# Block attention and feed-forward: another order of scores, attn*v and transposes in the pairs of batches 2 to 7

## The chip, the cores and the metric

The kernel runs on one core of one Trainium2 chip. The time is that of one execution on the device in microseconds (us); lower is better.

## The reference

Attention over q, k, v of 8 batches, 8 heads, 576 positions and 64 columns with a block mask (blocks of 64; a block sees itself and those before it), then a feed-forward part on all 4608 rows with 512 and 2048 columns. All is float32.

```python
scores = scale * np.matmul(q, k.transpose(0, 1, 3, 2))
mask = block_i >= block_j                     # block = position // 64
scores = np.where(mask, scores, -1000000000.0)
scores = scores - np.max(scores, axis=-1, keepdims=True)
attn = np.exp(scores)
attn = attn / (np.sum(attn, axis=-1, keepdims=True) + 1e-09)
x = np.matmul(attn, v)                        # then (B*S, H*D)
h = x @ w_in
g = np.where(h >= 1, h, np.where(h <= -1, 0.0, (h + 1) ** 2 / 4))
out = g @ w_out
```

## The kernel before

**Tiling.** Two heads make a pair, so there are 32 pairs, four to a batch. Each value is held as two float32r parts (high and low), and products are made of several matmuls of such parts. `q` and `k` of a pair are transposed on TensorE into `qa`, `qb`, `ka`, `kb` (`turned_raw`, L401, for the 512 main positions of one head; `turned_last`, L442, for the last 64 of both heads). `parted` takes four reads to split a bank of them (L388 ScalarE, L389 VectorE, L394 ScalarE, L395 VectorE); `turned_last` has two more on VectorE (L446).

**One pair.** `scores(j, g)` makes softmax rows of head j, group g (query tiles 0 and 1; 2; 3): matmuls L482 and L485 into a bank, the maximum L505 (VectorE), the exponential L509 (ScalarE), sum and reciprocal L491 and L492, and the scaling L515 into `pr`. `scores_last` does the last 64 rows of both heads. `as_float32r` then copies `pr` by DMA to `prr` in the float32r type (L250, queue SP). `turn(j, g)` transposes `prr` (L552), and `split` reads the bank twice (L545 ScalarE, L547 VectorE) into `pa` (group 0) or `pb`. `turn_last` does so for the last rows; their last 64 columns, the corner of P, have a transpose, a bank and two reads of their own, into `pcs`. attn*v are the matmuls L591: `attn_v_first` for the first 256 rows of both heads, `attn_v(0)` and `attn_v(1)` for the other 320 rows of one head. `add_halves` copies half of the bank to `xtmp` (L613 ScalarE) and adds the other (L614 VectorE) into `x32`, which `store_x` splits into `xh` and `xl` for the feed-forward part.

**Order.** `attention_steps` gives eight steps per pair, with `old`, `cur` and `nxt` the pair before, this one and the one behind. The pairs of batches 2 to 7 are `far`, `raw` and `hop`; those before are laid out otherwise. From step 36 on each attention step is followed by one step of `feed_forward`: `ffn_in` (twelve matmuls L770 of 512 columns into `ph`; then L779 ScalarE, L780 and L783 VectorE, L784 ScalarE, L785 GpSimd) in the odd steps 1, 3, 5, 7, and `ffn_out` (twelve matmuls L794 and L799) in the even ones. So the far pairs run, with what follows in each step:

| step | before, in the source's order | feed-forward |
|---|---|---|
| 0 | old.turn(1, 1), scores(0, 0), load v, old.attn_v_first | ffn_out |
| 1 | old.turn(1, 2), scores(0, 1), turned_last, fetch | ffn_in |
| 2 | old.attn_v(1), old.store_x, scores(0, 2) | ffn_out |
| 3 | begin, turn(0, 0), scores_last, nxt.load_qk | ffn_in |
| 4 | turn(0, 1), scores(1, 0), nxt QK of half 0 | ffn_out |
| 5 | turn(0, 2), scores(1, 1) | ffn_in |
| 6 | turn_last with the corner, scores(1, 2) | ffn_out |
| 7 | turn(1, 0), attn_v(0), nxt QK of half 1 | ffn_in |

**Banks.** PSUM has eight banks: four for `po`, one for `ph`, and in this stretch three for all the rest (`work_bank`, L85, `bufs=3`). Waits between engines are put in by the framework. It also lays out each engine's queue when the program is built, with the source's order as its guide; the trace shows where the two differ.

## Time and profile before

| | before |
|---|---|
| median of 3 runs | 1267.56 us (1264.57 to 1269.79) |
| the profiled execution | 1269.69 us, span 1267.9 us |
| mean granted TensorE clock | 0.981 of 2.4 GHz |
| busy: TensorE / VectorE / ScalarE / GpSimd | 95% / 70% / 55% / 31% |
| weight loads of TensorE | 79% |
| the 16 DMA engines | 54.9% for the data queue |

The far pairs take from about 262 to about 1075 us. From 1086 us on the feed-forward part runs alone. In the rows, PE is TensorE, DVE VectorE, ACT ScalarE, POOL GpSimd, SPq the SP queue that issues DMAs; L numbers are lines of the kernel. A matmul's row ends later than the next one's starts, since matmuls are pipelined; what a matmul costs the queue is the time from its start to the next start.

### The profile page before, as it was taken

The numbers are of one execution on the slowest core, as the hardware profiler recorded it, in microseconds if no ns is written. First come the engines' busy times: TensorE is split into PE (matmuls) and PEld (weight loads), VectorE is DVE, ScalarE is ACT, GpSimd is POOL, SyncE is SP. The second block draws the span as 40 slices with busy tenths as digits, with TensorE's granted clock in tenths as the row PEclk, the third lists the DMA queues.
The fourth block names the chain that finished last, engine by engine and source line by source line (L and its number), as shares of the span: only waits on it lengthen the run. The fifth ranks groups of instructions, "written<-read, shape, count | busy, mean of one in ns | idle before, by whom it ended". The sixth has DMA issues, their size and how long they took to land.

```text
span 1267.9 us, 20253 instructions
## 1 busy us (share of the span) xinstructions
PE 1200.1 (95%) x6280; PEld 998.8 (79%) x6280; DVE 887.0 (70%) x2188; ACT 703.2 (55%) x1827; POOL 394.6 (31%) x430
## 2 busy tenths in 40 slices
PE   5888889899999999999999999999999999999998
PEld 4666667678888888888888888888888888888886
DVE  8898877758777777777777777787777777322222
ACT  5787656646566655665656655566556555222222
POOL 3555655522222222222222222222222222222222
PEclk9888988999999999999999999999999999999999
DMA  5566666667888655555554655465556433422432
GB/s 158 167 176 215 203 228 197 217 198 237 260 273 266 215 162 158 154 175 163 156 162 145 187 157 152 138 189 153 160 154 190 137 128 118 132 87 98 133 100 100
DMA packets 185259, 215.43 MB, mean 170 GB/s; under 512 B 113840, under 2 KB 132272, under 8 KB 184384
## 3 DMA queue, kind: packets, MB, share of 16 engines
q1 hardware_dynamic: 185152, 214.14, 54.9%
q8 instruction: 50, 0.82, 0.3%
q14 instruction: 57, 0.47, 0.1%
HBM read 134.74 MB, written 31.98 MB: 131 GB/s over the span
## 4 chain that ended last, share of the span: by engine, by line
PE 69%; DVE 16%; ACT 6%; issue 5%; DMA 1%; POOL 1%; SPq 1%; ACTq 0%; POOLq 0%; DVEq 0%
PE ph L770 29%; PE po L794 15%; PE po L799 7%; PE ps_av L591 7%; PE ps_s L482 4%; ACT pr L509 3%; PE ps_s L485 3%; DVE t L780 2%; PE ps_t L552 2%; DVE t L783 2%; ACT t L779 2%; DVE pb L547 2%; DVE nm L505 2%; DVE sm L491 1%; DVE pr L515 1%
## 5 line engine op out<-in xcount | busy, mean ns | idle before, releaser
L785 POOL TENSOR_TENSOR gl<-t,gh 128x512 fp32r<-128x512 f32 x144 | 187.5, 1302 | 510.2 <-ACT gh L784 333.2
L794 PE MATMUL po<-wo,gh 128*128 128x512 f32 x1152 | 296.1, 397 | 0.5 <-DMA wo<-wo_split 0.3
L794 PEld LDWEIGHTS po<-wo,gh 128*128 128x128 f32 x1152 | 212.5, 189 | 44.5 <-DMA wo<-wo_split 0.7
L770 PE MATMUL ph<-xh,wih 128*128 128x512 f32 x576 | 232.9, 404 | 1.6 <-DVE t L783 1.6
L770 PE MATMUL ph<-xh,wil 128*128 128x512 f32 x576 | 228.8, 397 | 0.0
L770 PE MATMUL ph<-xl,wih 128*128 128x512 f32 x576 | 227.8, 396 | 0.5 <-DVE xl L627 0.5
L780 DVE SCALAR_TENSOR_TENSOR t<-t 128x512 f32<-128x512 f32 x144 | 101.5, 705 | 168.0 <-ACT t L779 165.2
L779 ACT ACTIVATE t<-ph 128x512 f32<-128x512 f32 x144 | 85.9, 597 | 173.8 <-PE ph L770 173.8
L509 ACT ACTIVATE pr<-ps_s,nm 128x128 f32<-128x128 f32 (+3 forms) x256 | 134.1, 527 | 60.5 <-DVE nm L505 58.4
L784 ACT CAST gh<-t 128x512 fp32r<-128x512 f32 x144 | 89.5, 621 | 120.3 <-DVE t L783 120.0
L799 PE MATMUL po<-wo,gl 128*128 128x512 f32 x576 | 155.6, 392 | 0.0
L482 PE MATMUL ps_s<-ka,qa 68*128 68x288 f32 (+4 forms) x384 | 135.3, 367 | 15.0 <-ACT pr L509 5.4
L379 POOL TENSOR_TENSOR vsr<-vn,vsr 128x256 fp32r<-128x256 f32 (+1 forms) x96 | 55.2, 576 | 246.2 <-ACT vsr L378 244.6
L770 PEld LDWEIGHTS ph<-xh,wil 128*128 128x128 f32 x576 | 109.5, 190 | 23.8
L770 PEld LDWEIGHTS ph<-xh,wih 128*128 128x128 f32 x576 | 109.8, 191 | 21.7 <-DVE t L783 2.3
L799 PEld LDWEIGHTS po<-wo,gl 128*128 128x128 f32 x576 | 108.7, 189 | 23.1
L505 DVE TENSOR_REDUCE nm<-ps_s 128x1 f32<-128x128 f32 (+3 forms) x256 | 118.8, 482 | 10.4 <-PE ps_s L485 9.4
L770 PEld LDWEIGHTS ph<-xl,wih 128*128 128x128 f32 x576 | 109.7, 190 | 20.5 <-DVE xl L627 0.9
L485 PE MATMUL ps_s<-kb,qb 128*128 128x288 f32 (+4 forms) x384 | 121.1, 322 | 0.0
L515 DVE TENSOR_SCALAR pr<-pr,sm 128x128 f32<-128x128 f32 (+3 forms) x256 | 107.3, 440 | 5.4
L783 DVE TENSOR_TENSOR t<-ph,t 128x512 f32<-128x512 f32 x144 | 98.7, 686 | 2.2
L491 DVE TENSOR_SCALAR sm<-sm 128x1 f32<-128x1 f32 (+1 forms) x224 | 52.0, 232 | 68.3 <-ACT pr L509 65.7
(111 smaller groups left out, 1871.4 us busy)
## 6 DMA issues: line engine op xcount, KB each, us to landing
wo<-wo_split SPq DMA_DIRECT2D x144, 512.0 KB, 3.5
prr<-pr SPq DMA_DIRECT2D x96, 192.0 KB, 2.5
prr<-pr SPq DMA_DIRECT2D x72, 256.0 KB, 2.8
out_dram<-ob SPq DMA_DIRECT2D x36, 256.0 KB, 2.9
bits<-in_moe_w_in_dram SPq DMA_DIRECT2D x32, 256.0 KB, 3.5
bits<-in_moe_w_out_dram SPq DMA_DIRECT2D x32, 256.0 KB, 3.0
wo_split<-ws SPq DMA_DIRECT2D x16, 512.0 KB, 2.9
qa<-qb SPq DMA_DIRECT2D x63, 128.0 KB, 2.4
```

The lines of the kernel that those rows point to most:

```text
L482: nc.tensor.matmul(ps, qa[:KA, j, c0 : c0 + P], ka[:KA, j, k0 : k0 + n], start=first, stop=False)
L485: nc.tensor.matmul(ps, qb[:, j, c0 : c0 + P], kb[:, j, k0 : k0 + n], start=False, stop=last)
L505: nc.vector.tensor_reduce(out=nm[:, i : i + 1], in_=ps[:, cs], axis=AX.X, op=ALU.max, negate=True)
L509: nc.scalar.activation(pr[:, cs], ps[:, cs], AF.Exp, bias=nm[:, i : i + 1], scale=1.0, accum_out=sm[:, i : i + 1],)
L515: nc.vector.tensor_scalar_mul(pr[:, cs], pr[:, cs], sm[:, i : i + 1])
L770: nc.tensor.matmul(ph, w[:, cc, fs], x[:, cc, xs], start=(cc == 0 and i == 0), stop=(cc == NCC - 1 and i == 2),)
L779: nc.scalar.activation(t_, ph, AF.Relu, bias=0.5, scale=0.5)
L780: nc.vector.scalar_tensor_tensor(out=t_, in0=t_, scalar=1.0, in1=t_, op0=ALU.min, op1=ALU.mult)
L783: nc.vector.tensor_tensor(out=t_, in0=ph, in1=t_, op=ALU.max)
L785: nc.gpsimd.tensor_tensor(out=gl, in0=t_, in1=gh.bitcast(F32), op=ALU.subtract)
L794: nc.tensor.matmul(po[tt], gh[:, ts_], wo[:, w, :], start=(fc == 0 and w == 0), stop=False)
L799: nc.tensor.matmul(po[tt], gl[:, ts_], wo[:, 0, :], start=False, stop=fc == NFC - 1)
```

## The change

For the pairs of batches 2 to 7 alone: in each step the scores come first, then the transposes or attn*v. `attn_v(0)` moves from step 7 to step 0 of the next pair, and `attn_v_first` from step 0 to step 1, with one `xtmp` for its two halves; `attn_v(1)` stays in step 2. `turned_last` of the next pair runs in step 5 and no more in the pair's own step 1. The corner of P is transposed in step 7 into the free columns of the bank of `turn(1, 0)`, and no more in step 6 into a bank of its own. The copy to `prr` is issued at the end of the step (`move`).

```diff
@@ -513,7 +513,18 @@
             self.inverse(sm[:, :m])
             for i, cs in enumerate(cols):
                 nc.vector.tensor_scalar_mul(pr[:, cs], pr[:, cs], sm[:, i : i + 1])
-            self.pr[j, g] = as_float32r(pr[:, : cols[-1].stop], self.plain) if self.hop else [pr]
+            self.pr[j, g] = [pr[:, : cols[-1].stop]]
+            if not self.far:
+                self.moved(j, g)
+
+        def moved(self, *key):
+            if self.hop:
+                self.pr[key] = as_float32r(self.pr[key][0], self.plain)
+
+        def move(self, *key):
+
+            if self.far:
+                self.moved(*key)
 
         def scores_last(self):
 
@@ -539,7 +550,9 @@
             nc.vector.tensor_tensor(out=sm[:, 2:3], in0=sm[:, 0:1], in1=sm[:, 1:2], op=ALU.add)
             self.inverse(sm[:, 2:3])
             nc.vector.tensor_scalar_mul(pr, pr, sm[:, 2:3])
-            self.pr["last"] = as_float32r(pr, self.plain) if self.hop else [pr]
+            self.pr["last",] = [pr]
+            if not self.far:
+                self.moved("last")
 
         def split(self, ps, hi, lo=None):
             nc.scalar.copy(hi, ps)
@@ -560,6 +573,8 @@
             ps = work_bank("ps_t")
             for c0 in range(0, n, P):
                 self.transposed(ps[:, c0 : c0 + P], pr, c0, P)
+            if self.far and j == 1 and g == 0:
+                self.turn_corner(self.pr.pop(("last",)), ps[:BLK, n : n + P])
             if g == 0:
                 self.split(ps[:, :n], *self.pa[j])
             else:
@@ -570,7 +585,7 @@
                 )
 
         def turn_last(self):
-            pr = self.pr.pop("last")
+            pr = self.pr["last",] if self.far else self.pr.pop(("last",))
             ps = work_bank("ps_t")
             for c0 in range(0, SM, P):
                 self.transposed(ps[:, c0 : c0 + P], pr, c0, P)
@@ -578,11 +593,13 @@
                 ps[:, :SM].rearrange("p (t h c) -> p t h c", h=2, c=BLK),
                 *(x[:, :, :, G1 - BLK :].rearrange("p h t c -> p t h c") for x in self.pb),
             )
-            ps = work_bank("ps_t")
-            self.transposed(ps[:BLK, :P], pr, SM, BLK)
-            self.split(
-                ps[:BLK, :P].rearrange("p (h c) -> p h c", h=2), *(x[:BLK] for x in self.pc)
-            )
+            if not self.far:
+                self.turn_corner(pr, work_bank("ps_t")[:BLK, :P])
+
+        def turn_corner(self, pr, ps):
+
+            self.transposed(ps, pr, SM, BLK)
+            self.split(ps.rearrange("p (h c) -> p h c", h=2), *(x[:BLK] for x in self.pc))
 
         def weighted(self, ps, j, parts, first=True, last=True):
             for i, (kt, lo_col, mov) in enumerate(parts):
@@ -605,11 +622,10 @@
                 parts.append((kt, lo_col, [x[:, j, kt, lo_col:] for x in self.pb]))
             return (*parts, (NTL, SM - G0, [x[:, j, :] for x in self.pc]))
 
-        def add_halves(self, ps, j, c0):
+        def add_halves(self, ps, j, c0, xtmp):
             main = slice(j * D, (j + 1) * D)
             rest = slice((1 - j) * D, (2 - j) * D)
             n = ps.shape[1]
-            xtmp = att1.tile([P, G1], F32, tag="xtmp", name="xtmp")
             nc.scalar.copy(xtmp[main, :n], ps[rest, :])
             nc.vector.tensor_tensor(
                 out=self.x32[main, c0 : c0 + n], in0=ps[main, :], in1=xtmp[main, :n], op=ALU.add
@@ -634,15 +650,16 @@
             ps = work_bank("ps_av")
             for j in range(2):
                 self.weighted(ps[:, j * G0 : (j + 1) * G0], j, self.parts_first(j))
+            xtmp = att1.tile([P, G1], F32, tag="xtmp", name="xtmp")
             for j in range(2):
-                self.add_halves(ps[:, j * G0 : (j + 1) * G0], j, 0)
+                self.add_halves(ps[:, j * G0 : (j + 1) * G0], j, 0, xtmp)
 
         def attn_v(self, j):
             if self.plain:
                 return self.both(G0, self.parts) if j else None
             ps = work_bank("ps_av")[:, :G1]
             self.weighted(ps, j, self.parts(j))
-            self.add_halves(ps, j, G0)
+            self.add_halves(ps, j, G0, att1.tile([P, G1], F32, tag="xtmp", name="xtmp"))
 
         def store_x(self):
 
@@ -675,82 +692,92 @@
             nxt = pairs[i + 1] if i + 1 < len(pairs) else None
             far = old is not None and old.far
             near = old is not None and not old.far
-            if far:
-                old.turn(1, 1)
             if cur:
                 cur.scores(0, 0)
                 cur.turned(False, 1)
                 cur.load("v")
             if far:
-                old.attn_v_first()
+                old.turn(1, 1)
+                old.attn_v(0)
             if near:
                 old.turn(1, 2)
+            if cur:
+                cur.move(0, 0)
             yield
+            if cur:
+                cur.scores(0, 1)
+                if not cur.raw:
+                    cur.turned_last()
+            if i + 2 < len(pairs):
+                pairs[i + 2].fetch()
             if far:
                 old.turn(1, 2)
-            if cur:
-                cur.scores(0, 1)
-                cur.turned_last()
-            if i + 2 < len(pairs):
-                pairs[i + 2].fetch()
+                old.attn_v_first()
             if near:
                 old.attn_v(1)
                 old.store_x()
+            if cur:
+                cur.move(0, 1)
             yield
             if far:
+                if cur:
+                    cur.scores(0, 2)
                 old.attn_v(1)
                 old.store_x()
-            if not cur:
-                return
-            if cur.far:
+                if not cur:
+                    return
+                if not cur.far:
+                    cur.begin()
+                    cur.turn(0, 0)
+            elif cur.far:
                 cur.scores(0, 2)
             else:
                 cur.begin()
                 cur.scores(0, 2)
                 cur.turn(0, 0)
+            cur.move(0, 2)
             yield
             if cur.far:
                 cur.begin()
+                cur.scores_last()
                 cur.turn(0, 0)
-                cur.scores_last()
             else:
                 cur.scores_last()
                 cur.turn(0, 1)
+            cur.move("last")
             if nxt:
                 nxt.load_qk()
                 nxt.split_q()
             yield
             if nxt:
                 nxt.split_k()
-            if cur.far:
-                cur.turn(0, 1)
-                cur.scores(1, 0)
-            else:
-                cur.scores(1, 0)
-                cur.turn(0, 2)
+            cur.scores(1, 0)
+            cur.turn(0, 1 if cur.far else 2)
+            cur.move(1, 0)
             if nxt:
                 nxt.turned(True, 0)
             yield
+            cur.scores(1, 1)
             if cur.far:
                 cur.turn(0, 2)
-                cur.scores(1, 1)
             else:
-                cur.scores(1, 1)
                 cur.turn_last()
+            cur.move(1, 1)
             if nxt:
                 nxt.turned(False, 0)
+                if nxt.raw:
+                    nxt.turned_last()
             yield
+            cur.scores(1, 2)
             if cur.far:
                 cur.turn_last()
-                cur.scores(1, 2)
             else:
-                cur.scores(1, 2)
                 cur.attn_v(0)
                 cur.turn(1, 0)
+            cur.move(1, 2)
             yield
             if cur.far:
                 cur.turn(1, 0)
-                cur.attn_v(0)
             else:
                 cur.turn(1, 1)
                 cur.attn_v_first()
```

## Rows read from the trace of the kernel before

**Rows 1.** Stretches (all pairs; one pair; its step 4; its steps 4 to 7): us, busy time by engine, granted clock.

```profile
262.00:1075.00 813.00, 798.63 (x4411) 675.79 (x4411) 619.98 (x1526) 482.78 (x1245) 213.36 (x224) 1.00 0.58 177
...
606.87:640.39 33.52, 32.84 (x183) 27.84 (x182) 25.64 (x64) 19.90 (x51) 8.83 (x9) 1.00 0.52 154
624.14:628.00 3.86, 3.86 (x24) 3.31 (x23) 3.46 (x7) 2.74 (x7) 0.42 (x1) 1.00 0.73 220
...
624.14:640.39 16.25, 15.95 (x90) 13.50 (x89) 12.82 (x29) 9.47 (x23) 2.90 (x3) 1.00 0.56 175
```

**Rows 2.** Waits: engine and line, whom it waited for, us in total, times, longest.

```profile
ACT kb L394 <- DVE qb L389: 22.8, 46, 0.8
...
PE ps_qk L442 <- DVE x L614: 8.9, 23, 0.4
...
PE ps_s L482 <- ACT pr L509: 5.4, 18, 0.3
```

**Rows 3.** Order of time, step 1: start, us, instruction, [idle before <- who ended it].

```profile
645.36 0.34 PE L485 MATMUL ps_s<-kb,qb 128*128 128x384 f32 x1
645.50 0.43 DVE L614 TENSOR_TENSOR x<-ps_av,xtmp 64x256 f32<-64x256 f32 x1
...
646.08 0.25 PE L442 MATMUL ps_qk<-ident_r,qk 128*128 128x128 f32 x1 [0.38 <-DVE x L614]
...
646.16 0.47 PE L770 MATMUL ph<-xh,wih 128*128 128x512 f32 x1
```

**Rows 4.** Order of time, TensorE, step 6.

```profile
631.54 0.51 PE L552 MATMUL ps_t<-ident_r,prr 128*128 128x128 f32 x5
632.35 0.50 PE L482 MATMUL ps_s<-ka,qa 68*128 68x512 f32 x1 [0.30 <-ACT pr L509]
```

**Rows 5.** Order of time, TensorE: scores behind L770, behind transposes; L770 behind transposes.

```profile
270.46 0.22 PE L482 MATMUL ps_s<-ka,qa 68*128 68x128 f32 x1
270.52 0.28 PE L485 MATMUL ps_s<-kb,qb 128*128 128x128 f32 x1
...
637.55 0.46 PE L770 MATMUL ph<-xh,wih 128*128 128x512 f32 x1
637.86 0.39 PE L770 MATMUL ph<-xl,wih 128*128 128x512 f32 x1
638.08 0.40 PE L770 MATMUL ph<-xh,wil 128*128 128x512 f32 x1
...
640.60 0.29 PE L482 MATMUL ps_s<-ka,qa 68*128 68x128 f32 x1
640.73 0.28 PE L485 MATMUL ps_s<-kb,qb 128*128 128x128 f32 x1
```

**Rows 6.** Order of time, the reads of QK half 0, step 4.

```profile
625.37 0.59 ACT L388 ACTIVATE qb<-ps_qk 64x512 fp32r<-64x512 f32 x1
...
627.35 0.69 DVE L389 SCALAR_TENSOR_TENSOR qb<-ps_qk,qb 64x512 fp32r<-64x512 f32 x1
...
629.71 0.69 DVE L395 TENSOR_TENSOR kb<-ps_qk,kb 64x512 fp32r<-64x512 f32 x1
```

**Rows 7.** Order of time, first and last read of QK half 1, step 7.

```profile
637.98 0.59 ACT L388 ACTIVATE qb<-ps_qk 64x512 fp32r<-64x512 f32 x1
...
639.94 0.69 DVE L395 TENSOR_TENSOR kb<-ps_qk,kb 64x512 fp32r<-64x512 f32 x1 [0.65 <-ACT kb L394]
```

**Rows 8.** Order of time, TensorE, step 6 of the first changed pair.

```profile
297.47 0.52 PE L552 MATMUL ps_t<-ident_r,prr 128*128 128x128 f32 x5
297.83 1.62 PE L794 MATMUL po<-wo,gh 128*128 128x512 f32 x6
299.42 0.50 PE L482 MATMUL ps_s<-ka,qa 68*128 68x512 f32 x1
```

**Rows 9.** Page, DMA issues: count, KB each, median us to landing.

```profile
prr<-pr SPq DMA_DIRECT2D x96, 192.0 KB, 2.5
```

**Rows 10.** Groups by line and shape: count | busy us, mean ns | idle before.

```profile
L395 DVE TENSOR_TENSOR kb<-ps_qk,kb 64x128 fp32r<-64x128 f32 x24 | 7.0, 293 | 0.7
```

## The prediction

> **What bounds the kernel now.** I read the page first, then the stretches, then who waited for whom, then the order of time in one pair. In the stretch that holds the 24 changed pairs TensorE is busy 98 of 100 us at granted clock 1.00 (2.4 GHz), VectorE 76, ScalarE 59 [rows 1]. One pair takes 33.52 us; what is outside that stretch the change hardly touches. So time moves only if TensorE's own queue moves: fewer or cheaper instructions on it, or fewer waits. Two waits of TensorE repeat there once per pair [rows 2]: the transpose of `turned_last` (L442) for the addition of `attn_v_first` (L614), and `scores(1, 2)` (L482) for an exponential (L509). Both are waits for a bank. The work banks are three and go round, so a bank asked for is the one asked for three requests earlier, and it has to be read out first.
>
> The first wait: TensorE starts the last matmul of `scores(0, 1)` at 645.36 and the transpose at 646.08, right after the addition that began at 645.50 (0.43 us long) [rows 3]. A matmul of 512 columns starts 0.22 to 0.23 after its forerunner [rows 5], so one of 384 needs some 0.17: 0.72 - 0.17 = 0.55 lost. The waits view gives 0.39 (8.9 / 23), counting from the modelled end of the matmul before; 0.72 would be all of it. 0.55 lies between. 24 x 0.55 = 13 us.
>
> The second: five transposes start at 631.54 and `scores(1, 2)` at 632.35 [rows 4]; five transposes need 0.36 (297.47 to 297.83 in [rows 8]). 0.81 - 0.36 = 0.45 lost, 18 times, 8 us. In the other six pairs six matmuls of the feed-forward part stand between, and 1.59 - 6 x 0.23 = 0.2 is lost [rows 8]: 1 us.
>
> **The change part by part.** *Removed.* The corner's bank is gone: step 6 asks for two banks, not three, and `scores(1, 2)`, now first, finds its bank asked for by `scores(1, 1)` a whole step earlier. `turned_last` leaves step 1. Both old waits should go: 13 + 8 + 1 = 22 us. The corner's transpose (one) and its two small reads remain, a step later.
>
> *Scores first.* A score matmul behind transposes costs more than one behind the feed-forward part: from L482 to L485 it takes 0.13 behind `turn`, 0.06 behind L770 [rows 5]. Seven of eight steps begin with scores afterwards: 7 x 0.07 = 0.49. The price goes over in part to what follows the transposes: the first feed-forward matmul behind transposes takes 0.31, its next 0.22 [rows 5], 0.09 more. Steps 2, 3, 5 and 6 had scores there and now have attn\*v or transposes, and in step 1 the weighted sum now follows transposes: at most 5 x 0.09 = 0.45, at least, where the step's end was no better before, 0.2. So 0.04 to 0.29 a pair; I take 0.2, nearer the upper end, since step 7 also loses the change from the weighted sum to transposes: 5 us. Removed in all: 27 us.
>
> *attn\*v in three steps.* `attn_v(0)` goes from step 7 to step 0 of the next pair, `attn_v_first` from step 0 to 1: the same matmuls at the same price. Their inputs are complete a step earlier than needed; `x32` is stored only behind `attn_v(1)` in step 2, as before. The tightest bank is that of `attn_v(0)`, asked for again by `attn_v_first` after twelve feed-forward matmuls, scores and transposes, some 3.5 us, with a copy and an addition of about 0.5 each to do: from 0 to little, taken as 0. But step 7 gets shorter on TensorE by eight matmuls of up to 320 columns at 0.14 (0.225 x 320 / 512) and two small ones, some 1.3 us, of which below.
>
> *The copy of P issued last (`move`).* It lands in 2.5 us [rows 9] and is read three steps later, some 12 us: hidden even if issued a step late. On SP's queue the loads now go ahead of the copy, which waits for VectorE; nothing there was late for TensorE. Each `move` takes a buffer that a `turn` of its own step or the one before has just read, so it waits no longer than TensorE's own order. Bound: from 0 to a step's delay, still covered; I take 0.
>
> *The corner in a shared bank.* Readers of one bank take turns: ScalarE's second read of the QK bank waited 46 times for VectorE's, 0.5 each [rows 2]. Two small reads of some 0.3 each [rows 10] with two handovers of 0.2 hold the bank of `turn(1, 0)` about 1 us longer. Its next user, `turn(1, 1)`, comes after 2.8 us of feed-forward matmuls and half a us of scores. From 0 to some 0.3 if VectorE is behind; I take 0 here and count that under "VectorE" below.
>
> *`turned_last` in step 5: the new wait.* In the new order the requests run `scores(1, 0)`, `turn(0, 1)`, QK of half 0 in step 4, `scores(1, 1)`, `turn(0, 2)`, `turned_last` in step 5. So `turned_last` gets the bank of QK half 0, asked for only some 3.5 us before. That bank is read four times in turn (L388, L389, L394, L395). Now these begin at 625.37 and the last ends at 629.71 + 0.69 = 630.40 [rows 6], 6.26 after the step's start at 624.14. Step 4 lasts 3.86 [rows 1], less 0.07; `scores(1, 1)` and `turn(0, 2)` need 0.36 and 0.29: TensorE is at `turned_last` 4.44 after the step's start. From above: 6.26 - 4.44 = 1.8 us a pair. From below: where nothing stood between, as in step 7, the same four reads took 637.98 to 640.63, 2.65 us [rows 7]; begun at 625.37 they end at 628.02, 3.9 after the step's start, ahead of 4.44: no wait. Behind the waiting transpose stand the twelve matmuls of that step's feed-forward part, and all else of TensorE.
>
> Between 0 and 1.8 I take 0.35. The nearest rows are the two old waits: the queue's order isn't always the source's. Where a bank came late, six feed-forward matmuls had been put ahead of `scores(1, 2)`, and 0.2 was lost; where the order stayed, 0.45 and 0.55 [rows 3, 4, 8]. A wait of 1.8 would be the largest repeated one, and I expect the order of the queue to fill it as there.
>
> This is where a rule speaks against the change. In the rows the transpose that waited held up the feed-forward matmul behind it: L770 starts only after L442 [rows 3]. The Trainium skill, "PSUM — Partial Sum Buffer", section "Engine vs sequencer instructions", says that matmuls start and complete in program order, so that no matmul passes one that waits. By that rule, with the source's order on the queue, the sum would hold 24 x 1.8 = 43 us of new waiting, the first rival below; by the row with the feed-forward matmuls put ahead, a few us.
>
> *VectorE in steps 4 to 7.* From 624.14 to 640.39 it is busy 12.82 of 16.25 us [rows 1]. The change adds four reads by VectorE of some 0.29 [rows 10] and takes away one addition of about 0.5 (0.43 for 256 columns, [rows 3]): 13.5. TensorE's share shrinks by 0.45 (the wait), 1.3 (`attn_v(0)`) and some 0.2: 14.3. VectorE goes from 79% to 94% of that stretch, and its 3.4 us of waiting for ScalarE must mostly be filled. Three banks let it fall behind by about a step's scores, 1.5 us. From 0 (all filled) to 13.5 + 3.4 - 14.3 - 1.5 = 1.1 a pair; I take 0.2 beyond the wait above, since a wait of TensorE gives VectorE the same time.
>
> The sum: 27 - 24 x (0.35 + 0.2) = 27 - 13 = 14 us less. The profiled execution took 1269.69 us, its span is 1267.9, and the median of the runs is 1267.56, 2.1 below it. 1269.7 - 14 - 2.1 = 1254 us.
>
> **The rivals.** *A: the new bank wait stands in full* (slower). The order stays the source's, `turned_last` waits 1.8 us in every pair: 24 x 1.8 - 27 = 16 us more, 1284. It outweighs the gain from 27 / 24 = 1.1 us a pair on. For it: the late L395 behind the softmax of `scores(1, 0)`; the old waits stayed in order 18 and 24 times. Against it: the softmax begins earlier, and [rows 8].
>
> *B: VectorE becomes the bound of steps 4 to 7* (no change). New waits of about 1 us a pair, spread over `turned_last`, `turn_last` and the banks of step 7: 27 - 24 = 3 us less, 1265, from 1261 to 1273. For it: 94%. Against it: VectorE's idle time now ends with waits for an exponential, and more work that is ready stands beside it.
>
> *C: no new wait at all*: 1267.6 - 27 = 1240. For it: the lower bounds above; against it: two tight places.
>
> **How the numbers follow.** Forecast 0.50, A 0.15, B 0.22, C 0.13. A measurement of this kernel can tell some 0.5%, 6 us, from no change: faster is below 1261, slower above 1274. Faster: forecast and C, less a spill over 1261: 0.62. Same: B and the spill: 0.23. Slower: A, 0.15. The range runs from C to the upper end of B, 1239 to 1275; only A lies outside. The forecast's own range is 1246 to 1261.
>
> **What would show it.** Right: no wait of `turned_last` for L614, no wait of `scores(1, 2)` for L509; a pair of about 33.52 - 0.6 = 32.9 us; L442 between feed-forward matmuls or a wait of it for L395 of under 0.5 us; from L482 to L485 0.06 for 128 columns. A: L442 waits 1 us or more for L395, 23 or 24 times, and a pair takes over 33.5. B: waits of TensorE at several places of steps 5 to 7, with VectorE over 90% busy there. Wrong altogether: a lower granted clock, waits of TensorE for a copy of P, or more time outside the 24 pairs.

## The result, and the profile after

| | before | after |
|---|---|---|
| median of 20 runs | 1267.96 us | 1272.21 us |
| lowest to highest | 1264.57 to 1270.02 | 1268.55 to 1275.81 |
| ratio to before, 95% interval | | 1.0035 [1.0026, 1.0044] |
| profiled execution, its span | 1269.69, 1267.9 us | 1272.54, 1270.8 us |

The change makes the kernel slower by 0.35%, some 4 us. The forecast was 14 us less. The time lies in the range and within the 0.5% counted as no change, but on the other side of zero. All that the change was to remove is gone; two things that it brought cost slightly more.

Line numbers move with the change: L552 of before is now L565, L591 is L608, L613 and L614 are L629 and L630, L770 is L797, L794 is L821, L545 and L547 (the two reads of `split`) are L558 and L560, L780 and L783 are L807 and L810, L785 is L812; lines up to L515 keep theirs. In the experiments some numbers move by a few lines once more: L773 and L794 below are the feed-forward matmul L797, L617 is the addition L630, L594 is the matmul L608. The page of the kernel after, busy time of the engines:

```profile
PE 1196.5 (94%) x6280; PEld 1001.2 (79%) x6280; DVE 922.1 (73%) x2188; ACT 702.7 (55%) x1827; POOL 395.2 (31%) x430
```

Stretches of the kernel after: an ordinary pair, the first pair of a chunk, then steps 4 to 7 of each (us; busy us of TensorE, its weight loads, VectorE, ScalarE, GpSimd; granted clock, DMA share, GB/s):

```profile
587.68:621.00 33.32, 32.59 (x183) 27.93 (x182) 26.90 (x63) 19.82 (x51) 8.90 (x10) 1.00 0.53 154
687.66:721.98 34.32, 32.93 (x184) 28.01 (x183) 28.74 (x65) 20.79 (x54) 9.52 (x11) 1.00 0.59 181
591.83:607.21 15.38, 14.65 (x81) 12.15 (x80) 14.02 (x32) 9.54 (x23) 2.59 (x2) 1.00 0.54 164
691.83:707.67 15.84, 14.81 (x81) 12.16 (x80) 14.84 (x33) 10.18 (x25) 2.59 (x2) 1.00 0.65 216
```

And the same two kinds of pair before the change:

```profile
586.76:620.23 33.47, 32.77 (x185) 27.82 (x184) 25.87 (x64) 19.90 (x51) 9.12 (x10) 1.00 0.51 154
687.22:720.45 33.23, 32.82 (x185) 27.71 (x184) 26.44 (x65) 20.77 (x54) 9.58 (x11) 1.00 0.60 186
```

This is the whole result in four rows. The clock is the same, 1.00 in every row. An ordinary pair went from 33.47 to 33.32, the first pair of a chunk (a chunk is the 512 rows that the feed-forward part takes at a time, four pairs long; six of the 24 are first ones, in which the four banks `po` of the chunk before are copied out) from 33.23 to 34.32, in some to 34.6, 34.4 on average. 18 x (33.32 - 33.47) + 6 x (34.4 - 33.23) = -2.7 + 7.0 = 4.3 us: the measured difference.

Inside the ordinary pair, the waits of TensorE between 262 and 1075 us (engine, line, whom it waited for; us in total, times, longest):

```profile
PE ps_qk L442 <- DVE kb L395: 14.9, 21, 0.8
PE ps_qk L401 <- ACT pr L509: 2.7, 6, 0.7
PE ps_av L608 <- DVE kb L395: 2.0, 6, 0.4
```

Neither wait of [rows 2] is left, not that of L442 for the addition of `attn_v_first` and not that of `scores(1, 2)` for an exponential. In their place L442, the transpose of `turned_last`, waits for L395, the last read of the bank of QK half 0. The order of time in steps 4 and 5 of the kernel after shows why (start, us, instruction, idle before):

```profile
591.83 0.22 PE L482 MATMUL ps_s<-ka,qa 68*128 68x128 f32 x1
591.89 0.28 PE L485 MATMUL ps_s<-kb,qb 128*128 128x128 f32 x1
...
593.08 0.59 ACT L388 ACTIVATE qb<-ps_qk 64x512 fp32r<-64x512 f32 x1
...
595.04 0.69 DVE L389 SCALAR_TENSOR_TENSOR qb<-ps_qk,qb 64x512 fp32r<-64x512 f32 x1
...
595.75 0.58 ACT L394 CAST kb<-ps_qk 64x512 fp32r<-64x512 f32 x1
...
596.32 0.47 PE L797 MATMUL ph<-xh,wih 128*128 128x512 f32 x1
...
596.55 0.55 DVE L515 TENSOR_SCALAR pr<-pr,sm 128x128 f32<-128x128 f32 x2
...
596.62 0.39 PE L797 MATMUL ph<-xl,wih 128*128 128x512 f32 x1
596.85 0.40 PE L797 MATMUL ph<-xh,wil 128*128 128x512 f32 x1
597.14 0.69 DVE L395 TENSOR_TENSOR kb<-ps_qk,kb 64x512 fp32r<-64x512 f32 x1
...
597.98 0.25 PE L442 MATMUL ps_qk<-ident_r,qk 128*128 128x128 f32 x1 [0.72 <-DVE kb L395]
598.06 0.46 PE L797 MATMUL ph<-xh,wih 128*128 128x512 f32 x1
```

The four reads run in turn, L388, L389, L394, L395, and each of VectorE's stands behind other work of its queue (L389, free to run at 593.67, behind feed-forward, softmax and `split`; L395, free at 596.33, behind L515): L389 starts 3.21 us after the step's start, as it did before (627.35 - 624.14, [rows 6]), and L395 ends at 597.83, 6.0 after it. By the source's order TensorE would be at L442 at 596.32, 4.49 after the step's start: 1.5 too early. The queue has three feed-forward matmuls put ahead (596.32 to 597.08 with the last one's 0.23), which hides 0.76. The rest, 597.08 to 597.98, is lost: 0.9 us. Over the trace the time between the starts of that feed-forward matmul and L442 is too long 23 times, by 0.87 each: 20 us, nearly the 22 of the old waits. The matmul behind L442 follows 0.08 after it and not before: nothing passes the transpose that waits. That matmuls start and complete in program order is the rule of the Trainium skill, "PSUM — Partial Sum Buffer", section "Engine vs sequencer instructions", that the prediction weighed; the trace agrees with it here.

In the first pair of a chunk two more waits come on top, the second and the third row of the waits above. Its order of time, with two of the four copies of `po` that steps 5 and 6 hold, and the two places that wait:

```profile
698.30 0.57 ACT L834 COPY ob<-po 128x512 f32<-128x512 f32 x1
698.30 0.69 DVE L836 COPY ob<-po 128x512 f32<-128x512 f32 x1
...
704.50 0.53 PE L401 MATMUL ps_qk<-ident_r,qk 128*128 128x128 f32 x4 [0.43 <-ACT pr L509]
...
705.09 1.29 POOL L812 TENSOR_TENSOR gl<-t,gh 128x512 fp32r<-128x512 f32 x1 [8.81 <-PE ps_qk L401]
...
705.35 1.31 DVE L515 TENSOR_SCALAR pr<-pr,sm 128x512 f32<-128x512 f32 x1
...
708.03 0.69 DVE L395 TENSOR_TENSOR kb<-ps_qk,kb 64x512 fp32r<-64x512 f32 x1
...
708.86 0.82 PE L608 MATMUL ps_av<-pb,vsr 128*128 128x320 f32 x4 [0.36 <-DVE kb L395]
```

VectorE has two copies of 0.69 (the first at 696.2) to fit into a stretch where it is already busy 14.02 of 15.38 us; here it is busy 14.84 of 15.84, 94%, and the last read of QK half 1 (708.03) has slipped behind the end of the stretch. In the same six pairs L515 of 512 columns, beside GpSimd's L812, takes 1.30 to 1.32, where the same one of an ordinary pair takes 0.49; it stands right ahead of the reads L389 and L395, and no run takes it away by itself. The exponential for which QK half 1 waits (L401) and the last read for which `attn_v(0)` waits (L608) both come late; between starts 0.61 and 0.5 are lost, six times each.

### The profile page after: what moved, and what is told of

Same layout as the page of the kernel before. It is cut to its first block, busy times and chain, and to the rows that moved or that the text cites. A ratio compares the mean times of both kernels' runs of the same rounds, so it can differ in the third digit from the quotient of the medians.

```text
span 1270.8 us, 20177 instructions
## 1 busy us (share of the span) xinstructions
PE 1196.5 (94%) x6280; PEld 1001.2 (79%) x6280; DVE 922.1 (73%) x2188; ACT 702.7 (55%) x1827; POOL 395.2 (31%) x430
## 5 line engine op out<-in xcount | busy, mean ns | idle before, releaser
L812 POOL TENSOR_TENSOR gl<-t,gh 128x512 fp32r<-128x512 f32 x144 | 192.6, 1338 | 612.4 <-issue 193.3
L821 PE MATMUL po<-wo,gh 128*128 128x512 f32 x1152 | 298.9, 400 | 0.2
L797 PE MATMUL ph<-xh,wih 128*128 128x512 f32 x576 | 239.2, 415 | 1.8 <-DVE t L810 1.8
L821 PEld LDWEIGHTS po<-wo,gh 128*128 128x128 f32 x1152 | 208.8, 189 | 40.2 <-DMA wo<-wo_split 0.8
L797 PE MATMUL ph<-xl,wih 128*128 128x512 f32 x576 | 228.8, 397 | 0.5 <-DVE xl L643 0.5
L797 PE MATMUL ph<-xh,wil 128*128 128x512 f32 x576 | 228.6, 397 | 0.0
L807 DVE SCALAR_TENSOR_TENSOR t<-t 128x512 f32<-128x512 f32 x144 | 101.4, 704 | 163.5 <-ACT t L806 161.5
L509 ACT ACTIVATE pr<-ps_s,nm 128x128 f32<-128x128 f32 (+3 forms) x256 | 133.8, 526 | 36.6 <-DVE nm L505 27.1
L505 DVE TENSOR_REDUCE nm<-ps_s 128x1 f32<-128x128 f32 (+3 forms) x256 | 123.8, 486 | 25.4 <-PE ps_s L485 22.7
L482 PE MATMUL ps_s<-ka,qa 68*128 68x288 f32 (+4 forms) x384 | 122.4, 333 | 9.2 <-ACT kb L427 4.6
L797 PEld LDWEIGHTS ph<-xh,wil 128*128 128x128 f32 x576 | 110.2, 191 | 24.9
L797 PEld LDWEIGHTS ph<-xh,wih 128*128 128x128 f32 x576 | 109.6, 190 | 21.1 <-DVE t L810 2.2
L515 DVE TENSOR_SCALAR pr<-pr,sm 128x128 f32<-128x128 f32 (+3 forms) x256 | 121.9, 496 | 4.6
L797 PEld LDWEIGHTS ph<-xl,wih 128*128 128x128 f32 x576 | 110.1, 191 | 19.3 <-DVE xl L643 0.8
L810 DVE TENSOR_TENSOR t<-ph,t 128x512 f32<-128x512 f32 x144 | 98.7, 685 | 2.0
L379 POOL TENSOR_TENSOR vsr<-vn,vsr 128x256 fp32r<-128x256 f32 (+1 forms) x96 | 50.5, 527 | 143.7 <-ACT vsr L378 137.5
L482 PEld LDWEIGHTS ps_s<-ka,qa 68*128 68x128 f32 x384 | 74.7, 195 | 20.1 <-ACT kb L427 5.1
```

What stands on the lines that cost most here:

```text
L482: nc.tensor.matmul(ps, qa[:KA, j, c0 : c0 + P], ka[:KA, j, k0 : k0 + n], start=first, stop=False)
L505: nc.vector.tensor_reduce(out=nm[:, i : i + 1], in_=ps[:, cs], axis=AX.X, op=ALU.max, negate=True)
L509: nc.scalar.activation(pr[:, cs], ps[:, cs], AF.Exp, bias=nm[:, i : i + 1], scale=1.0, accum_out=sm[:, i : i + 1],)
L515: nc.vector.tensor_scalar_mul(pr[:, cs], pr[:, cs], sm[:, i : i + 1])
L797: nc.tensor.matmul(ph, w[:, cc, fs], x[:, cc, xs], start=(cc == 0 and i == 0), stop=(cc == NCC - 1 and i == 2),)
L807: nc.vector.scalar_tensor_tensor(out=t_, in0=t_, scalar=1.0, in1=t_, op0=ALU.min, op1=ALU.mult)
```

## The experiments

Two theories stand against each other. One says that the loss is the bank of QK half 0, asked for too early by `turned_last` in step 5. The other says that VectorE is too full in steps 4 to 7, so that a wait taken from `turned_last` comes up elsewhere. Where an expectation speaks of theory 1 and theory 2 and says no more, they are these two, in this order. All runs have the kernel before beside them on the same chip (1267.58 to 1268.12 us).

**`turned_last` back in step 1**, behind `scores(0, 1)`; all else as changed.

```diff
                 cur.scores(0, 1)
-                if not cur.raw:
-                    cur.turned_last()
+                cur.turned_last()
...
                 nxt.turned(False, 0)
-                if nxt.raw:
-                    nxt.turned_last()
```

> The changed kernel with one part undone: turned_last of a pair runs in its own step 1 again, right behind scores(0, 1), and no more in step 5 of the pair before. Theory 1 (bank): the changed kernel loses because turned_last takes the bank of QK half 0, which is still being read; TensorE waits there 0.9 us in each of 24 pairs (L442 for L395). Here it takes the bank of turn(1, 1), long read out: no wait of L442, some 20 us less than the changed kernel, about 1252 us. Theory 2 (VectorE): VectorE is the bound of steps 4 to 7. The four reads of 0.29 us leave that stretch, 1.1 us a pair, but TensorE goes on waiting for VectorE at the banks of step 7: 5 to 12 us less, about 1263 us.

Measured: 1249.96 us, ratio 0.9859 [0.9837, 0.9882]. Its ordinary pair and the first of a chunk, then its longest repeated wait of TensorE in the changed pairs:

```profile
578.59:611.07 32.48, 32.48 (x183) 27.91 (x182) 26.24 (x63) 20.10 (x51) 8.94 (x10) 1.00 0.51 155
675.91:709.15 33.24, 32.76 (x183) 27.89 (x182) 28.78 (x65) 21.18 (x54) 9.44 (x11) 1.00 0.60 187
```

```profile
PE ps_t L565 <- DVE pb L560: 2.2, 5, 0.7
```

The one request moved is worth 22 us. The ordinary pair falls by 0.84, the wait of 0.87, and in it TensorE is busy without a gap (32.48 of 32.48). The wait did not come up elsewhere in them, though VectorE has the same work per pair in less time. Four of its reads have left steps 4 to 7, however, so this run alone does not part the two theories; the next two do. The first pairs of the chunks stay 0.76 longer than the others.

**The reads of the QK bank in another order**: both of ScalarE, then both of VectorE, so that the bank changes hands once and not three times; `turned_last` stays in step 5.

```diff
             nc.scalar.mul(hi, ps[:D], SCALE)
+            nc.scalar.copy(khi, ps[D:])
             nc.vector.scalar_tensor_tensor(
...
-            nc.scalar.copy(hi, ps[D:])
-            nc.vector.tensor_tensor(out=lo, in0=ps[D:], in1=hi.bitcast(F32), op=ALU.subtract)
+            nc.vector.tensor_tensor(out=klo, in0=ps[D:], in1=khi.bitcast(F32), op=ALU.subtract)
```

> The changed kernel, but the bank of transposed q and k is read in the order ScalarE, ScalarE, VectorE, VectorE, not ScalarE, VectorE, ScalarE, VectorE: the same four instructions. Theory 1 (bank): the bank of QK half 0 is free over 1 us sooner, since ScalarE's second read needs not wait for VectorE's first; L442's wait of 0.9 us a pair falls under 0.2, 15 to 20 us less than the changed kernel, about 1254 us. Theory 2 (VectorE): VectorE has the same work, so it ends as late: under 4 us less, about 1270 us.

Measured: 1254.02 us, 0.9897 [0.9877, 0.9916]. The wait of L442 in its view of waits (the weight-load side of TensorE), where the kernel after has 25.4 us for L797:

```profile
PEld ps_qk L442 <- PE ps_t L565: 4.7, 23, 0.2
```

L442 stands right behind the transposes of `turn(0, 2)` again (L565, not L797), and VectorE's work is what it was. The bank is out sooner, though still not in time: L442 starts 0.15 behind the end of L395 as before, and between starts 0.25 is lost where it was 0.87, 23 times, 6 us. So the position in step 5 is bad above all for a bank with four reads that alternate.

**`turned_last` in step 6**, where the ring gives it another bank.

```diff
             cur.move(1, 2)
+            if nxt and nxt.raw:
+                nxt.turned_last()
```

> The changed kernel with turned_last of the next pair in step 6, behind turn_last, not in step 5: it takes the bank of turn(0, 2). VectorE's work in steps 4 to 7 is the same. Theory 1 (bank): no wait of L442 for L395, 15 to 20 us less than the changed kernel, about 1254 us. Theory 2 (VectorE): the wait moves to the banks of step 7 and of the next step 0 and is about as long: within 4 us of the changed kernel, about 1270 us.

Measured: 1253.83 us, 0.9892 [0.9871, 0.9913]. An ordinary pair takes 32.37, a first one 34.1 to 34.2 (34.45 once). VectorE's work in steps 4 to 7 is the same as with the change, and L442 no longer waits: the bank theory is right for the 18 ordinary pairs. The six first pairs lose almost as much as with the change.

**Before, with `turned_last` moved to step 5 alone.**

```diff
                 cur.scores(0, 1)
-                cur.turned_last()
+                if not cur.raw:
+                    cur.turned_last()
...
                 nxt.turned(False, 0)
+                if nxt.raw:
+                    nxt.turned_last()
```

> The kernel before with one part of the change alone: turned_last in step 5, behind scores(1, 1). The old wait of L442 for L614, 13 us, goes. Theory 1 (bank): turned_last now takes the bank of QK half 0 here too; TensorE gets there 28.7 us after the same zero where the bank is free at 630.4 less 600, so 1.7 us late, of which matmuls put ahead hide some 0.7: a wait of about 1 us a pair, 24 us. In all about 10 us slower than before, 1278 us. Theory 2 (VectorE): VectorE has idle time in the old order (79% busy), so the wait stays small: 8 to 12 us faster than before, about 1258 us.

Measured: 1274.32 us, 1.0054 [1.0035, 1.0074]. Its waits, TensorE's and then its weight loads':

```profile
PE ps_qk L442 <- DVE kb L395: 10.3, 15, 0.7
...
PEld ps_qk L442 <- PE ph L773: 21.3, 23, 1.1
PEld ps_s L482 <- issue: 12.9, 23, 0.6
```

The new wait comes with this one part, without the rest of the change: 0.84 at L442, 17 times, in place of the old 0.55. `scores(1, 2)`, still behind the corner's bank, goes on losing 0.32, now in 23 pairs. Ordinary pairs take 33.6, first ones 33.7, against 33.47 and 33.23 before.

**Before, with the corner in the shared bank alone.**

```diff
+            if self.far and j == 1 and g == 0:
+                self.turn_corner(self.pr.pop("last"), ps[:BLK, n : n + P])
...
-            ps = work_bank("ps_t")
-            self.transposed(ps[:BLK, :P], pr, SM, BLK)
+            if not self.far:
+                self.turn_corner(pr, work_bank("ps_t")[:BLK, :P])
```

> The kernel before with one part of the change alone: the corner of P is transposed in step 7 into the free columns of the bank of turn(1, 0). If the wait of scores(1, 2) for an exponential (0.45 us, 18 times) came from the corner's bank alone: that wait goes, 8 us less than before, 1260 us, and the wait of L442 for L614 stays at 13 us. Rival: readers of one bank take turns, so the shared bank is held some 1 us longer and attn_v(0) in the same step 7 needs the corner: TensorE waits there as long as before at scores(1, 2), 1267 us.

Measured: 1266.63 us, 0.9988 [0.9974, 1.0003]. Its waits of TensorE:

```profile
PE ps_qk L442 <- DVE x L617: 9.0, 22, 0.6
...
PE ps_av L594 <- DVE pcs L547: 1.7, 6, 0.3
```

The wait of `scores(1, 2)` (0.45 a pair) is gone, but `attn_v(0)`, still in step 7, now has its corner read out late and loses 0.32 between starts in 23 pairs (the view of waits counts six of them). By this the shared bank pays only together with `attn_v(0)` a step later: that move, which I had put at nothing, would be worth 0.32 x 23 = 7 us beside this one. No run has these two parts alone.

**The change, with all four copies of `po` on ScalarE.**

```diff
-            if tt % 2:
-                nc.scalar.copy(ob, po[tt])
-            else:
-                nc.vector.tensor_copy(ob, po[tt])
+            nc.scalar.copy(ob, po[tt])
```

> The changed kernel with the four copies of po (end of each chunk, in step 5 of every fourth pair) all on ScalarE, not two on ScalarE and two on VectorE. In the changed kernel those pairs take 1.0 to 1.3 us more than the others. If VectorE's load in steps 4 to 7 is the cause: 1.2 us less for VectorE there, the six pairs come down to about the others, 5 us less than the changed kernel, 1267 us. Rival: the wait is for ScalarE's exponentials (L401 waits for L509 in those pairs), which now queue behind two more copies of 0.6 us: the six pairs get longer, 1274 to 1278 us.

Measured: 1268.56 us, 1.0005 [0.9992, 1.0018], against 1.0035 [1.0026, 1.0044] for the change. An ordinary pair and a first pair:

```profile
652.65:685.97 33.32, 32.60 (x183) 27.92 (x182) 26.88 (x63) 19.82 (x51) 8.89 (x10) 1.00 0.51 154
685.97:719.60 33.63, 32.82 (x184) 27.98 (x183) 27.80 (x63) 21.83 (x56) 9.52 (x11) 1.00 0.59 184
```

The ordinary pair stands still, the first falls from 34.4 to 33.6: VectorE's two copies are most of what the first pairs lose. In five of the six the long L515 is still there (1.58 to 1.59), and `attn_v(0)` loses 0.27; in the other one it takes 0.49, and `attn_v(0)` does not wait.

**Step 1 again, and the copies on ScalarE** (the first experiment with the edit of the last one).

> The change with turned_last in step 1 again (the best kernel so far, 1249.96 us, its ordinary pair 32.48, the first pair of each chunk 33.24) and the four copies of po all on ScalarE. Theory 1 (the copies cost VectorE its room, and only in the first pairs of the chunks): ordinary pairs stay at 32.5, the six first pairs fall by about 0.5 each, as from 33.43 to 32.9 with the parted reads in the other order: 6 x 0.5 = 3 us less, 1247. Theory 2 (ScalarE gets in the way of other pairs): the ordinary pairs rise by 0.1 and the time stays at 1250 or goes above.

Measured: 1245.1 us, 0.9823 [0.9804, 0.9842], the fastest kernel of all. An ordinary pair and a first pair:

```profile
510.87:543.30 32.43, 32.43 (x183) 27.89 (x182) 26.21 (x63) 20.08 (x51) 8.90 (x10) 1.00 0.51 155
543.30:575.66 32.36, 32.36 (x183) 27.90 (x182) 27.15 (x63) 22.01 (x55) 8.66 (x10) 1.00 0.64 196
```

TensorE is busy in the whole of each pair, and the first pairs are no longer than the others: 33.24 - 32.36 = 0.88 each, 5.3 us, where 3 were expected. No wait of TensorE repeats in the 24 pairs any more, though L515 takes 1.5 in the six first pairs here too: nothing waits behind it there. Against before that is, over the 24 pairs, 18 x 1.06 + 6 x 0.85 = 24 us, beside 1268.12 - 1245.1 = 23.

**Step 6, and the copies on ScalarE.**

> The change with turned_last in step 6 (1253.83 us, ordinary pair 32.37, first pair of a chunk 34.1 to 34.2) and the four copies of po all on ScalarE. Theory 1: VectorE's load is what the first pairs lose; moving two copies away took 0.75 a pair from the change itself, so 6 x 0.75 = 4.5 us less here, 1249, first pairs at 33.4, ordinary pairs unchanged at 32.4. Theory 2: in step 6 turned_last itself holds a bank that the first pairs miss; then they stay above 34 and the time at 1253 or more.

Measured: 1249.26 us, 0.9861 [0.9836, 0.9886]. The first pairs fall from 34.2 to 33.1 (6 x 1.1 = 6.6, 4.6 measured), ordinary ones stay at 32.37. Such a pair:

```profile
542.58:575.69 33.11, 32.73 (x183) 28.09 (x182) 27.52 (x63) 21.57 (x55) 8.59 (x10) 1.00 0.61 187
```

A wait of 0.54 between starts ahead of `attn_v(0)`, for L395, remains in the six first pairs, and the run before, which differs in the place of `turned_last` alone, does not have it. So both theories have a part here: the copies most of it, that place a rest.

**Step 1 again, but transposes ahead of the scores in steps 3 to 6**, as in the kernel before; this undoes "scores first" there.

```diff
+            if cur.far:
+                cur.turn(0, 1)
             cur.scores(1, 0)
-            cur.turn(0, 1 if cur.far else 2)
...
-            cur.scores(1, 1)
             if cur.far:
                 cur.turn(0, 2)
-            else:
+            cur.scores(1, 1)
```

> The changed kernel with turned_last in step 1 as in the run before (about 1250 us), and in steps 3, 4, 5 and 6 the transposes ahead of the scores again. It measures the term for scores first. By the rows of the kernel before, each such step costs 0.07 us more at the scores, and 0.09 less at the first feed-forward matmul in steps 3, 5 and 6 only: 4 x 0.07 - 3 x 0.09 = 0 per pair, within 2 us of that run, unless a bank wait comes back. Rival: scores first is worth its place because the exponential starts sooner and frees its bank sooner; then scores(1, 1) or the QK transposes wait, 0.3 us or more a pair, 7 us more or above.

Measured: 1259.74 us, 0.9935 [0.9915, 0.9954], 10 us more than with scores first (7 in the profiled executions). Two waits come up, in its view of waits:

```profile
PE ps_av L608 <- DVE kb L395: 4.8, 17, 0.4
PE ps_t L565 <- DMA prr<-pr: 3.6, 6, 0.9
```

The first is 0.44 between starts, 17 times: 7.5 us. The second, for a copy of P, falls into the six first pairs, but these are no longer than with scores first (33.24 and 33.30 on average), where they wait elsewhere. So the order of scores and transposes is worth its place through the reads that have to end first, not through what a matmul costs behind another kind.

**Step 1 again, but attn\*v in two steps** (`attn_v_first` in step 0, `attn_v(0)` in step 7, as before).

```diff
                 old.turn(1, 1)
-                old.attn_v(0)
+                old.attn_v_first()
...
                 old.turn(1, 2)
-                old.attn_v_first()
...
                 cur.turn(1, 0)
+                cur.attn_v(0)
```

> The changed kernel with turned_last in step 1 (about 1250 us), and attn*v in two places again: attn_v(0) in step 7, attn_v_first in step 0. It measures what attn*v in three steps is worth. If TensorE has no other waits, the order of these matmuls costs nothing: within 2 us of that run. Rival: with attn_v(0) in step 7 three banks are asked for there; the transposes of QK half 1 then take the bank of turn_last or attn*v waits for the corner in the same step: 0.3 us or more a pair, 7 us more or above.

Measured: 1280.4 us, 1.0099 [1.0078, 1.0119]: 30 us more, where next to nothing was expected. Step 1 of an ordinary pair, in order of time:

```profile
615.80 0.22 PE L442 MATMUL ps_qk<-ident_r,qk 128*128 128x128 f32 x1
616.17 0.36 ACT L629 COPY xtmp<-ps_av 64x256 f32<-64x256 f32 x1 [0.80 <-DVE x L630]
616.62 0.43 DVE L630 TENSOR_TENSOR x<-ps_av,xtmp 64x256 f32<-64x256 f32 x1
...
617.15 0.51 PE L565 MATMUL ps_t<-ident_r,prr 128*128 128x128 f32 x4 [1.13 <-issue]
```

`turn(1, 2)` starts right behind the second addition of `attn_v_first`, whose bank it takes: 617.15 - 615.80 = 1.35 for one transpose of 0.06 to 0.08, so about 1.29 lost, 22 times, 28 us. The two copies and two additions of that bank run in turn, and in the new order of the step the bank is asked for early. It is the addition that L442 waited for in the kernel before ([rows 3]); here another transpose asks for its bank. With attn\*v in three steps, and `turned_last` in step 1 as here, nothing waits for it: in the change that old wait is gone through the three steps, and moving `turned_last` away was not needed for that.

**Step 1 and the other order of reads together**, then **the copies on ScalarE as well** (the edits shown above).

> The changed kernel with turned_last in step 1 and with the bank of q and k read in the order ScalarE, ScalarE, VectorE, VectorE. If TensorE has nothing left to wait for in an ordinary pair (32.45 us with turned_last in step 1), the sooner bank is worth nothing there: within 2 us of 1250 us. Rival: VectorE is still late in steps 4 to 7, and the bank that is free sooner gives 0.1 us or more a pair: 1247 us or less.

> The run before, and the four copies of po all on ScalarE. In the changed kernel that took 3.7 us off. If the first pair of each chunk is the only place left where TensorE waits (33.2 to 33.5 us against 32.45), it comes down by 0.5 to 0.8 in six pairs: 3 to 5 us less than the run before, 1246 us. Rival: there TensorE waits for turn_last's bank behind ScalarE, and two more copies on ScalarE make it longer: 1250 us or more.

Measured: 1256.91 us, 0.9914 [0.9896, 0.9931], and 1255.63, 0.9899 [0.9882, 0.9917]. Both missed: with `turned_last` in step 1 the new order of reads costs 7 to 10 us. Stretches of the second, an ordinary and a first pair, then two of its matmuls in step 1:

```profile
615.25:647.84 32.59, 32.59 (x183) 27.87 (x182) 25.74 (x63) 20.17 (x51) 9.09 (x10) 1.00 0.55 161
680.46:713.32 32.86, 32.74 (x184) 27.94 (x183) 27.28 (x63) 22.19 (x56) 9.42 (x11) 1.00 0.63 190
```

```profile
640.49 0.39 PE L794 MATMUL ph<-xh,wil 128*128 128x512 f32 x1
640.88 0.84 PE L608 MATMUL ps_av<-pa,vsr 128*128 128x256 f32 x5
```

A feed-forward matmul stands ahead of `attn_v_first`, as in the runs with step 1 alone, and 0.39 pass to the next start where without this order of reads it is 0.23: 0.17 a pair, 4 us. The bank of `attn_v_first` is that of `scores(0, 1)`, whose exponential (L509) here ends 0.06 ahead of the start. The rest of the difference was not settled.

## Why the prediction went wrong, and where it was right

**Right.** The two old waits, their sizes and their causes: with all new waits away (step 1, and the copies on ScalarE), the ordinary pair is 1.0 to 1.1 shorter, against 0.55 + 0.45 in the prediction. Right were also the place of the new wait, the bank and the instruction that ends it; the bounds of its lateness (1.8 put, 1.5 found; L395's end 6.26 and 6.0 after the step's start, TensorE's arrival 4.44 and 4.49); that the queue would have feed-forward matmuls ahead of L442; VectorE's share (94% put, 91% found in ordinary pairs); the copy of P and the granted clock, at no cost. The handover between two readers of a bank, put at 0.2, is 0.02 in the rows above (L389 ends at 595.73, L394 starts at 595.75); it did not enter the sum.

**The step that failed**: "Between 0 and 1.8 I take 0.35." It is 0.87 to 0.9. I reasoned that a queue that had filled a late bank once, with six matmuls, would fill this one. It took three, worth 0.76 of 1.5. That is 23 x 0.87 = 20 us where 24 x 0.35 = 8 stood in the sum. Nothing in the rows said that it would be six again: with three to six matmuls of 0.23 against a lateness of 1.5 to 1.8 the term lies between 0.1 and 1.1, and rival A (from 1.1 on) was a neighbour of the forecast, not a far case. The argument that the softmax begins earlier did not help: L505 and L509 of the earlier scores stand ahead of the bank's reads on the same two engines, and L389 starts 3.21 after the step's start in both kernels.

**The step that was missing**: the first pairs of the chunks. The prediction took all 24 pairs as one. In six of them VectorE has two copies of 0.69 more, and its full stretch of steps 4 to 7 has no room for them and for the L515 that comes out 0.8 longer there; 7 us. It is rival B's mechanism, in a quarter of the pairs, at 1.1 to 1.2 a pair, where 0.2 stood in the sum for every pair. The rows of before show these pairs only as slightly shorter ones (33.23).

**Terms that were mis-sized.** "Scores first", 0.2 a pair: the 0.13 that goes down to 0.06 is there (591.83 to 591.89), but the price passes to the next kind of matmul (596.32 to 596.62), and in ordinary pairs 0.02 to 0.06 is left of it: 33.47 - 0.55 - 0.45 + 0.87 = 33.34, and 33.32 was measured; 33.48 - 1.00 = 32.48, and 32.42 on average with step 1 and the copies on ScalarE. That is 3 to 4 us less than put. attn\*v in three steps, put at nothing: undone it costs 30 us, and it is what removes the first old wait. The corner alone: it needs `attn_v(0)` moved too.

In all: 22 us of old waits and some 1 to 2 us of scores first went, 20 us came with L442 and 7 with the first pairs: 3 to 4 us more, and 4 were measured. The forecast's 1254 is about what a single edit gives that takes the wait of L442 away, or most of it: 1250 to 1254. The edit that takes the first pairs' new cost alone gives 1268.6. That the time lay inside the range was in part luck: the range's upper end was rival B's, but the waits that came have other places and sizes than B's.

**What stays open.** Why the queue is filled with three matmuls and not six. What the order of reads costs beyond 0.17 a pair where `turned_last` is in step 1. How far VectorE's longer instructions (below) add to the waits, in the first pairs above all.

## What to carry to other kernels

Where a few banks go round, price a moved step by the request that stood one turn of the ring earlier: count when that bank's last read ends, from the step's start, and subtract when the matmul engine arrives; only whole matmuls that are ready at that place hide the difference. A bank with reads by two engines in turn should not be asked for again a step later; where it must be, let one engine read it after the other (0.25 in place of 0.87), but not elsewhere, where that order cost 7 to 10 us. And sum over kinds of pair: the few with extra work on the second busiest engine pay when the others just fit.

## What the runs showed of the hardware

VectorE's busy time rose from 887 to 922 us with the same count of instructions, 2188. The normalization of P with 384 columns, by line and shape, after:

```profile
L515 DVE TENSOR_SCALAR pr<-pr,sm 128x384 f32<-128x384 f32 x64 | 40.7, 636 | 1.8
```

and before:

```profile
L515 DVE TENSOR_SCALAR pr<-pr,sm 128x384 f32<-128x384 f32 x64 | 30.9, 482 | 1.6
```

The same 64 instructions take 636 ns on average instead of 482; that is 10 of the 35 us. One of them, beside a GpSimd instruction that had just begun, in the order of time after:

```profile
614.43 0.74 POOL L379 TENSOR_TENSOR vsr<-vn,vsr 128x256 fp32r<-128x256 f32 x1 [2.26 <-ACT vsr L378]
614.50 0.88 DVE L515 TENSOR_SCALAR pr<-pr,sm 128x384 f32<-128x384 f32 x1
```

It takes 0.88 where one with GpSimd idle takes 0.42, and ends 0.21 after GpSimd does. In the chunk's first pair above, L515 with 512 columns takes 1.31 beside L812 (mean before: 558 ns). In the 24 changed pairs 23 of these 384-column instructions find GpSimd running, and take 878 ns, and 25 do not, and take 421. The Trainium skill, "SBUF — State Buffer", section "Who interferes with whom", has VectorE share a pair of ports with GpSimd. An instruction of VectorE in a mode that uses both ports, which it says a `tensor_scalar` can enter, contends for the pair; whoever issued first holds it for the whole instruction while the other waits. In these rows the later one loses, with 0.88 against 0.42; which mode L515 runs in, no run here shows, nor that it stood still all the time (0.21 behind GpSimd's end is less than 0.42, and spans on GpSimd are rough). Another 10 of the 35 us are in L544, a minimum of two single columns: 186 ns on average before (there L533), 490 after. One that meets GpSimd:

```profile
588.63 1.42 POOL L674 TENSOR_TENSOR xl<-x,xh 128x576 fp32r<-128x576 f32 x1
...
589.46 0.62 DVE L544 TENSOR_TENSOR nm<-nm 128x1 f32<-128x1 f32 x1
```

It ends 0.03 behind GpSimd's instruction. A moved step can so make another engine slower without adding an instruction to it.
